# The last 256 rows' layernorm, issued between the older rows' down products

## The chip, the cores and the metric

The kernel runs on one core of one Trainium2 chip. The metric is the device time of a run in microseconds (us), given as a median over runs; less is better. The profile is one execution recorded by the hardware profiler. Its engines are called PE (TensorE matmul), PEld (TensorE weight load), DVE (VectorE), ACT (ScalarE), POOL (GpSimd) and SP (SyncE, which issues the DMAs of this kernel; SPq is its queue).

## The reference

One transformer block over 2048 rows of width 640, in bf16: a layernorm, attention with 32 heads of width 20, a residual, a second layernorm, a gated bilinear MLP of width 1728, and a second residual.

```python
def _layernorm(x, axis=-1, eps=1e-5):
    m = jnp.mean(x, axis=axis, keepdims=True)
    v = jnp.var(x, axis=axis, keepdims=True)
    return (x - m) / jnp.sqrt(v + eps)

h  = x + attention(_layernorm(x), A_wqkv, A_wo)   # 32 heads, softmax over 2048 keys
ln = _layernorm(h)
h2 = h + ((ln @ B_w_gate) * (ln @ B_w_up)) @ B_w_down
```

## The kernel before

**Tiling.** Rows go in blocks of 512 (four blocks, numbered 0 to 3), each of four tiles of 128 rows. Attention fills most of the span: score products on PE, exponentials on ACT (with a share of them done on DVE), value products on PE. A planner written in Python fills the gaps of that stream with jobs: projections, output products, and for the older rows the second layernorm and the MLP. It is a generator per job; a job yields between pieces of work, and the planner keeps clocks of its own to decide where a piece goes. The order is fixed when the program is built: each engine then runs its own list of instructions in that order.

**The end.** When the attention of block 3 is done, what is left cannot be spread over gaps any more. Its rows come in two halves: tiles 0 and 1 ("the older rows" here, 256 rows) are ahead, and tiles 2 and 3 (`LAST_T`, 256 rows) are last, since their attention ends last. The function `last_tail` (L1334) writes out the end by hand, after a pool `fin` of five PSUM buffers of one bank each (the tiles named `f`) has been opened. In the kernel before its steps are:

1. For each of the two last tiles, output products with the residual put in by an identity matmul (`out_most`, L1344 and L1346, `out_last`, L1350), into four `f` buffers. Between them the last head group is normalised (L793, L808, L1359).
2. For each of the two tiles, ACT copies the sums to SBUF (L1368), DVE takes mean and variance (`bn`, L219 and L220), and `rstd_act` (L921 to L934) makes the scale: small DVE instructions, a square root on ACT (L929), a reciprocal on DVE (L933).
3. `fill()` (L1383) runs what the planner has left. Here that is `job_y` of the older rows (L1272): four sets of 14 down products each (two row tiles by two halves of 320 columns; the matmuls are recorded at the helper `by_cols`, L286). Each set ends with one DVE addition to the residual (L1284), and after the second half of a tile a store of the tile goes out through SP's queue (L1291).
4. `ln_apply` (L243) on DVE subtracts the mean and scales, for both last tiles, giving the tiles `ln`.
5. `job_T` (L319) for both: five 128x128 transposes on PE (L323) into one `f` buffer, and one copy on ACT (L255) to `ln2T`.
6. Two weight tiles, `E`, are loaded through SP's queue (`w_tile`, L1187) for the MLP's third slice of columns; the other slices lie in SBUF or were asked for earlier.
7. `job_glu` (L1223) makes the MLP's up and gate products of the last rows (L1214, 140 matmuls, in slices 3, 4, 5, 6, 0, 1, 2); ACT copies up (L255), DVE multiplies it with gate (L1246, L1239) into `hh`. `flag` (L1388) checks the softmax sums.
8. `job_y` of the last rows: again four sets of 14 down products, four additions, and four stores of half a tile (L1289).

An `f` buffer is taken anew each time by `bank()` (L311), in turn; its taker waits until the reader of its last contents is done.

The helper that step 3 calls:

```python
    def fill():
        while peek() is not None:
            if cur["need"] != WAIT:
                run_slot()
```

`peek` (L509) tells whether a job is left, and `run_slot` (L537) runs one piece of it up to the point where its PSUM bank is closed, so that one call of `run_slot` is one set of 14 down products with its addition.

Of the kernel before, what the change touches and what calls it, by code (L numbers as in the profile page):

```python
# [87 lines left out]
def kernel(  # L88
# [91 lines left out]
    fill = []  # L180
# [61 lines left out]
    def ln_apply(dst, src, m32, r, k):  # L242
        nc.vector.tensor_scalar(dst, src, m32[:, k:k + 1], r[:, k:k + 1], ALU.subtract, ALU.mult)  # L243
# [9 lines left out]
    def evac(eng, dst, src):  # L253
        if eng == "act":
            nc.scalar.copy(dst, src)  # L255
        else:
            nc.vector.tensor_copy(dst, src)  # L257
# [19 lines left out]
    def mm(ns, kind="cols"):  # L277
        to(kind)
        clk["pe"] += ns
        clk["piece"] = ns  # L280
# [10 lines left out]
    def ev(n, slot=None):  # L291
        dve_op(n / 0.96 + 75, clk["pe"] + 150)
        slot = ring["cur"] if slot is None else slot
        ring["free"][slot] = clk["dve"] + WAKE
        if ring["busy"] == slot:
            ring["busy"] = None
# [7 lines left out]
    def ring_tile(dt=F32, w=BANK):  # L304
        k = ring["cur"] = next_slot()
        ring["order"].remove(k)
        ring["order"].append(k)
        clk["pe"] = max(clk["pe"], ring["free"][k])
        return mip.tile([P, w], dt, name="mi", tag=f"mi{k}")

    def bank(dt=F32, w=BANK):  # L311
        if end["pool"] is None:
            ps = ring_tile(dt, w)
            held["slot"] = ring["busy"] = ring["cur"]
            return ps
        ps = end["pool"].tile([P, BANK], F32, name="f", tag="f")
        return ps if dt == F32 else ps[:].bitcast(dt)[:, 0:w]

    def job_T(ln, dst, eng="dve", given=None, after=None):  # L319
        yield 60 * KT  # L320
        ps = bank(BF16, D) if given is None else given
        for c in range(KT):
            nc.tensor.transpose(ps[:, c * P:(c + 1) * P], ln[:, c * P:(c + 1) * P], ident[:])  # L323
        mm(60 * KT, "turn")
        if after:
            after()
        evac(eng, dst, ps[:].rearrange("p (c k) -> p c k", k=P))
        if given is None:
            ev(D // 2, held["slot"])
# [117 lines left out]
    for s, (p, g, lo, hi, _) in enumerate(segs):  # L447
        n = BANK // PASS[p][2]
# [50 lines left out]
    def advance():  # L499
        try:  # L500
            v = next(cur["gen"])
        except StopIteration:
            done.add(cur["key"])
            cur.update(key=None, gen=None, need=None, mid=False)
            return
        cur["mid"] = v is None
        cur["need"] = v

    def peek():  # L509
        if cur["mid"]:  # L510
            return 0
        if urgent and not (cur["key"] and cur["key"][0] == "nf"):
            if cur["gen"] is not None:
                jobs.appendleft((cur["key"], cur["gen"], cur["need"]))
            cur["key"], cur["gen"], cur["need"] = urgent.popleft()
        while cur["need"] is None or cur["need"] == WAIT:
            if cur["gen"] is None:
                if not jobs:
                    return None
                cur["key"], cur["gen"], cur["need"] = jobs.popleft()  # L520
                if cur["need"] not in (None, WAIT):
                    continue
            advance()
            if cur["need"] == WAIT:
                if cur["key"][0] == "nf" and jobs and not forced["on"]:
                    urgent.appendleft((cur["key"], cur["gen"], WAIT))
                    cur["key"], cur["gen"], cur["need"] = jobs.popleft()
                    continue
                other = None if forced["on"] else next((j for j in jobs if j[0] in needs and needs[j[0]] <= done), None)
                if other is None:  # L530
                    return WAIT
                jobs.remove(other)
                jobs.appendleft((cur["key"], cur["gen"], WAIT))
                cur["key"], cur["gen"], cur["need"] = other
        return cur["need"]

    def run_slot(limit=None):  # L537
        advance()
        while cur["mid"] and (limit is None or clk["pe"] <= limit):
            advance()  # L540
# [248 lines left out]
    def sums_to_rows(asb, w, ps=None):  # L789
        n = w // SLOT  # L790
        ps = bank() if ps is None else ps
        for t in range(w // P):
            nc.tensor.matmul(ps[:, HPG * t:HPG * (t + 1)], lhsT=asb[:, t * P:(t + 1) * P], rhs=late["if"][:, DH:P:SLOT], start=True, stop=True)  # L793
        mm(400, "turn")
        rr = nrm.tile([P, 2, NS], F32, name="rr", bufs=3)
        r16, ri = rr[:, 0, 0:n], rr[:, 1, 0:n]
        nc.vector.reciprocal(ri, ps[:, 0:n])
        bc = bc_tile(w)
        nc.vector.tensor_copy(bc[:, 0:w].rearrange("p (j e) -> p j e", e=SLOT), ri.rearrange("p (j e) -> p j e", e=1).to_broadcast([P, n, SLOT]))
        nc.vector.tensor_copy(r16, ps[:, 0:n])  # L800
        note_sums(rr, n)
        ev(w, held["slot"])
        return bc

    def rows_to_cols(bc, w, ps=None):
        ps = bank() if ps is None else ps
        for t in range(w // P):
            nc.tensor.matmul(ps[:, t * P:(t + 1) * P], lhsT=bc[:, t * P:(t + 1) * P], rhs=late["if"][:], start=True, stop=True)  # L808
        mm(800, "turn")
        return ps  # L810
# [373 lines left out]
    def w_tile(src, fp, wt):  # L1184
        w = min(FPW, FF - fp * FPW)
        view = wt[:, 0:KT * FPW].rearrange("p (c f) -> p c f", f=FPW)
        nc.sync.dma_start(view[:, :, 0:w], src[:, fp * FPW:fp * FPW + w].rearrange("(c p) f -> p c f", p=P))  # L1187
        return view
# [141 lines left out]
    def run(gen):  # L1330
        for _ in gen:
            pass

    def last_tail():  # L1334
        st = tail_st[LAST_B]
        on = On[LAST_B % 2]
        asb = final["asb"]
        c0 = LAST_T[0] * P
        ps_h = {}

        def out_most(t, hf):
            ps = ps_h[t, hf] = bank()
            cs = slice(hf * HALF, (hf + 1) * HALF)
            nc.tensor.matmul(ps[:, 0:HALF], lhsT=ident[:], rhs=st["xr"][t][:, cs], start=True, stop=False)  # L1344
            for g in range(NG - 1):
                nc.tensor.matmul(ps[:, 0:HALF], lhsT=on[g][:, t * P:(t + 1) * P], rhs=wo[g][:, cs], start=False, stop=False)  # L1346

        def out_last(t):
            for hf in range(2):
                nc.tensor.matmul(ps_h[t, hf][:, 0:HALF], lhsT=on[NG - 1][:, t * P:(t + 1) * P],  # L1350
                                 rhs=wo[NG - 1][:, hf * HALF:(hf + 1) * HALF], start=False, stop=True)
        ta, tb = LAST_T
        out_most(ta, 0)
        bc = sums_to_rows(asb, HW, ring_tile())
        out_most(ta, 1)
        ps = rows_to_cols(bc, HW, ring_tile())
        for k in range(2):
            cs = slice(k * P, (k + 1) * P)
            nc.vector.tensor_tensor(on[NG - 1][:, c0 + k * P:c0 + (k + 1) * P], asb[:, cs], ps[:, cs], ALU.mult)  # L1359
        out_most(tb, 0)  # L1360
        out_last(ta)
        out_most(tb, 1)
        out_last(tb)
        got = {}
        for t in LAST_T:
            mv = small.tile([P, 1, 2], F32, name="mv")
            for hf in range(2):
                nc.scalar.copy(st["xr"][t][:, hf * HALF:(hf + 1) * HALF], ps_h[t, hf][:, 0:HALF])  # L1368
            bn(mv, 0, None, [ps_h[t, hf][:, 0:HALF] for hf in range(2)])
            got[t] = rstd_act(mv, 1)  # L1370
        fill()
        ls = {}
        for t in LAST_T:
            ls[t] = late["s"].tile([P, D], BF16, name="ln2")
            ln_apply(ls[t][:], st["xr"][t][:], *got[t], 0)
        for t in LAST_T:
            run(job_T(ls[t], st["ln2T"][:, :, t * P:(t + 1) * P], "act"))
        st["w", 2] = [w_tile(src, 2, e_tile(0)) for src in (B_w_up, B_w_gate)]
        run(job_glu(st, LAST_T, tuple(range(RES0, FP)) + tuple(range(RES0))))
        flag()  # L1380
        run(job_y(st, LAST_T, True))

    def fill():  # L1383
        while peek() is not None:
            if cur["need"] != WAIT:
                run_slot()

    def flag():  # L1388
        le = dp.tile([P, DW], I16, name="dt", bufs=2)[:].bitcast(BF16)[:, 0:2 * NS]
# [171 lines left out]
```

## Time and profile before

| what | value |
|---|---|
| median of 3 runs | 879.17 us |
| lowest, highest run | 877.38 us, 884.9 us |
| span of the profiled execution (first to last instruction) | 875.8 us |
| PE, ACT, DVE busy over the span | 827.1, 799.6, 701.5 us |
| PE from 820 to 868 us, the end of the program | 44.17 of 48.00 us busy |

No time of its own is listed for the profiled execution beside its span; what lies around the span is in the runs' times and not in the profile. The median run stands 3.4 us above the span.

How to read it: the rows of the timeline give the start in us from the span's start, the length in us, the engine, the line, the operation with output and input, and the count of merged instructions; in square brackets stands how long the engine was idle before and which instruction ended that. The chain of work that ended last is followed back from the end: each row is a stretch in which that engine's work, or an "issue" gap, held the end. In a table by stretches, PEclk is the clock that was granted to TensorE as a share of full speed, and the DMA columns are the share of the 16 DMA engines and GB/s.

### The profile page before, as it was taken

The page shows a single profiled execution, that of the slowest core. Times are in us where ns is not written, and L with a number is a line of the kernel's source. Part 1 is how long each engine was busy: PE and PEld are TensorE (multiplying, and loading weights), DVE is VectorE, ACT ScalarE, POOL GpSimd, SP SyncE. Part 2 cuts the span into 40 slices and gives each one's busy share as a digit, 9 for nine tenths or more (in the row PEclk, how much of TensorE's full clock was granted, in tenths as well). Part 3 has the DMA queues.
Part 4 walks back from the last instruction along what each step waited for, and adds up shares of the span by engine and source line. Part 5 has one row for each costly group of instructions (what it writes and reads, how often), then busy time and mean ns, then how long its engine had stood idle before and what let it go on. Part 6 is the DMA issues. An engine that isn't in the chain of part 4 may idle for free.

```text
span 875.8 us, 34459 instructions
## 1 busy us (share of the span) xinstructions
PE 827.1 (94%) x15313; PEld 406.3 (46%) x15313; DVE 701.5 (80%) x1384; ACT 799.6 (91%) x711; POOL 191.0 (22%) x259
## 2 busy tenths in 40 slices
PE   8899999998999999999999999999999999999995
PEld 5334334332334334445444555655454556555774
DVE  6675778899778989888888888989988898788632
ACT  5899999999999999999999999999999999899530
POOL 2220001344413322212230223122310232014000
PEclk9999999999999999999999999999999999899998
DMA  6111230144222322101314031413510310031310
GB/s 183 35 59 52 68 98 3 44 120 114 53 67 53 115 74 76 39 9 39 98 40 128 24 98 45 117 31 97 127 34 23 99 48 15 17 93 48 82 46 18
DMA packets 93959, 57.62 MB, mean 66 GB/s; under 512 B 24236, under 2 KB 91692, under 8 KB 93804
## 3 DMA queue, kind: packets, MB, share of 16 engines
q1 hardware_dynamic: 93804, 55.36, 23.7%
q8 instruction: 121, 1.98, 0.9%
q14 instruction: 34, 0.28, 0.1%
HBM read 46.94 MB, written 8.16 MB: 63 GB/s over the span
## 4 chain that ended last, share of the span: by engine, by line
PE 46%; ACT 25%; DVE 19%; issue 5%; DMA 2%; SPq 1%; POOL 1%; ACTq 0%; DVEq 0%; POOLq 0%
ACT E L732 25%; PE sc L724 11%; PE acc L871 9%; PE mi L286 9%; PE mi L1214 8%; DVE di L744 5%; PE mi L360 3%; DVE di L632 2%; DVE dm L627 2%; DVE st L219 2%; PE f L286 2%; PE f L1214 2%; DVE dt L629 2%; PE mi L724 1%; PE acc L1421 1%
## 5 line engine op out<-in xcount | busy, mean ns | idle before, releaser
L732 ACT ACTIVATE E<-sc 128x1536 bf16<-128x1536 f32 (+1 forms) x679 | 782.5, 1271 | 23.6 <-PE sc L724 10.6
L744 DVE TENSOR_SCALAR di<-mi 128x512 int16<-128x512 f32 x350 | 238.1, 685 | 65.9 <-PE mi L724 61.8
L871 PE MATMUL acc<-E,vx 128*32 128x256 bf16 (+1 forms) x2532 | 221.4, 315 | 2.6 <-DVE vx L257 2.0
L724 PE MATMUL sc<-qa,kT 21*128 21x256 bf16 (+1 forms) x1800 | 205.2, 320 | 15.0 <-ACT E L732 10.1
L724 PEld LDWEIGHTS <-kT 21*128 21x128 bf16 x3072 | 85.6, 92 | 218.9 <-issue 208.7
L769 POOL TENSOR_TENSOR rr<-rr,powers 128x8 f32<-128x8 f32 (+1 forms) x44 | 95.9, 2180 | 407.0 <-DMA rr<-sums 406.9
L871 PEld LDWEIGHTS <-vx 128*32 128x32 bf16 x3612 | 81.5, 95 | 105.7 <-issue 95.0
L632 DVE TENSOR_TENSOR di<-di,dm 128x1024 bf16<-128x1024 bf16 x175 | 122.2, 698 | 4.6
L724 PE MATMUL mi<-qa,kT 21*128 21x256 bf16 (+1 forms) x376 | 98.0, 311 | 2.4 <-DVE di L744 1.3
L627 DVE TENSOR_SCALAR dm<-di 128x1024 int16<-128x1024 int16 x175 | 77.7, 444 | 3.7
L871 PE MATMUL acc<-dt,vx 128*32 128x256 bf16 (+1 forms) x540 | 78.1, 311 | 0.5 <-DVE dt L629 0.4
L871 PE MATMUL acc<-di,vx 128*32 128x256 bf16 (+1 forms) x540 | 77.8, 308 | 0.8 <-DVE di L632 0.6
L629 DVE TENSOR_SCALAR dt<-di 128x1024 int16<-128x1024 int16 x175 | 76.2, 436 | 0.0
L724 PE MATMUL sc<-qb,kT 21*128 21x256 bf16 (+1 forms) x732 | 67.1, 291 | 2.8 <-ACT E L732 2.4
L286 PE MATMUL mi<-wd,hh 128*32 128x320 bf16 x1344 | 63.5, 305 | 0.4 <-DVE hh L1239 0.2
L1214 PE MATMUL mi<-ln2T,wg 128*32 128x256 bf16 (+1 forms) x1170 | 55.6, 298 | 1.9 <-DVE di L744 1.0
L1214 PE MATMUL mi<-ln2T,wu 128*32 128x256 bf16 (+1 forms) x1170 | 54.6, 298 | 0.9 <-DVE di L744 0.5
L286 PEld LDWEIGHTS <-hh 128*32 128x32 bf16 (+1 forms) x1456 | 46.1, 98 | 18.0 <-issue 7.5
L1214 PEld LDWEIGHTS <-wg 128*32 128x32 bf16 (+1 forms) x1190 | 32.6, 96 | 13.7 <-issue 10.0
L286 PE MATMUL mi<-kT,ident 128*32 128x512 bf16 x528 | 37.0, 382 | 1.7 <-DVE di L744 1.6
L1214 PEld LDWEIGHTS <-wu 128*32 128x32 bf16 (+1 forms) x1190 | 32.4, 96 | 13.3 <-issue 9.3
L257 DVE CAST u<-mi 128x512 bf16<-128x512 f32 x49 | 33.5, 683 | 4.9 <-PE mi L1214 4.8
(134 smaller groups left out, 794.1 us busy)
## 6 DMA issues: line engine op xcount, KB each, us to landing
wu<-in_B_w_up_dram SPq DMA_DIRECT2D x29, 320.0 KB
wg<-in_B_w_gate_dram SPq DMA_DIRECT2D x29, 320.0 KB
dense<-dn SPq DMA_DIRECT2D x36, 128.0 KB
bc<-scr SPq DMA_DIRECT2D x64, 64.0 KB
bc<-scr SPq DMA_DIRECT2D x112, 32.0 KB
xr<-in_A_x_dram SPq DMA_DIRECT2D x16, 160.0 KB
out_dram<-xr SPq DMA_DIRECT2D x14, 160.0 KB
wd<-in_B_w_down_dram SPq DMA_DIRECT2D x13, 160.0 KB
```

What stands on the lines that cost most here:

```text
L257: nc.vector.tensor_copy(dst, src)
L286: nc.tensor.matmul(out[k:k + w, :], lhsT=lhsT[:, k:k + w], rhs=rhs, **flags)
L360: nc.tensor.matmul(ps[k:k + SLOT, :], lhsT=wqk_half(c, col // HALF)[:, m, col % HALF:col % HALF + SLOT], rhs=lnT[:, c, ch * QB:(ch + 1) * ...
L627: nc.vector.tensor_scalar(m16[:, 0:n], s16, M_MASK, M_BITS, ALU.bitwise_and, ALU.bitwise_or)
L629: nc.vector.tensor_scalar(t16[:, 0:n], s16, E_MASK, E_BITS, ALU.bitwise_and, ALU.bitwise_or)
L632: nc.vector.tensor_tensor(sb[:, 0:n], sb[:, 0:n], mb[:, 0:n], ALU.mult)
L724: nc.tensor.matmul(dst[:, h * w:(h + 1) * w], lhsT=kT[g][SLOT * j:SLOT * j + VS, (kt + h) * P:(kt + h + 1) * P], rhs=q_of(g, b, c0, w)[SLO ...
L732: nc.scalar.activation(e[:, 0:n], sc[:, 0:n], ACT.Exp, bias=EXP_BIAS, scale=SM_SCALE)
L744: nc.vector.tensor_scalar(t[:, k * BANK:(k + 1) * BANK], sd[:], EXP_A, 0.0, ALU.mult, ALU.max)
L769: nc.gpsimd.tensor_tensor(ri, r16, powers[:, 1:2].to_broadcast([P, n]), ALU.pow)
L871: nc.tensor.matmul(acc["t"][SLOT * j:SLOT * (j + 1), 0:w], lhsT=vx[kt][:, VS * h:VS * h + SLOT], rhs=e, start=(j not in acc["new"]), stop= ...
L1214: nc.tensor.matmul(ps[r0 + x:r0 + x + d, col:col + n], lhsT=wt[:, c, f0 + x:f0 + x + d], rhs=st["ln2T"][:, c, c0:c0 + n], start=(c == 0), ...
```

## The change

`fill` gets an optional count of pieces, and `last_tail` calls it three times: one set of the older rows' down products, then `ln_apply` for both last tiles, then two more sets, then the transposes of both last tiles with their ACT copies, then the rest, which is the fourth set. Nothing is computed otherwise, and no instruction is added or removed (DVE's list shows one row more only because four like rows in a row are split).

```diff
-        fill()
+        fill(1)
         ls = {}
         for t in LAST_T:
             ls[t] = late["s"].tile([P, D], BF16, name="ln2")
             ln_apply(ls[t][:], st["xr"][t][:], *got[t], 0)
+        fill(2)
         for t in LAST_T:
             run(job_T(ls[t], st["ln2T"][:, :, t * P:(t + 1) * P], "act"))
+        fill()
         st["w", 2] = [w_tile(src, 2, e_tile(0)) for src in (B_w_up, B_w_gate)]
...
-    def fill():
-        while peek() is not None:
+    def fill(n=None):
+        while n != 0 and peek() is not None:
             if cur["need"] != WAIT:
                 run_slot()
+                n = n and n - 1
```

On DVE, at the end of the two last tiles' statistics, with the old order marked - and the new one + (`xr` are the residual rows, `f` the PSUM buffers, `m` and `rstd` mean and scale, `hh` the MLP's product):

```order
 L927 TENSOR_SCALAR ve<-mvb 128x1
 L933 RECIPROCAL rstd<-den 128x1
-L1284 TENSOR_TENSOR xr<-f,xr 128x320 x4
-L243 TENSOR_SCALAR ln_21330<-xr,m_21239,rstd 128x640
-L243 TENSOR_SCALAR ln_21332<-xr,m_21256,rstd 128x640
+L1284 TENSOR_TENSOR xr<-f,xr 128x320
+L243 TENSOR_SCALAR ln_21280<-xr,m_21239,rstd 128x640
+L243 TENSOR_SCALAR ln_21282<-xr,m_21256,rstd 128x640
+L1284 TENSOR_TENSOR xr<-f,xr 128x320 x3
 L1246 TENSOR_TENSOR hh_19383<-f,u 128x2x256
```

The two `ln` instructions moved from behind the four additions to behind the first.

On PE, the kernel before, from the last product of the fourth set to the MLP's first product, each wait in brackets (`wd` is the down weight, `wres` an up or gate weight that lies in SBUF):

```order
L286 MATMUL f<-wd_5233,hh_19386 128x320
L323 LDWEIGHTS ln_21330 [waits DVE_49]
L323 MATMUL f<-ident,ln_21330 128x128
...
L323 MATMUL f<-ident,ln_21332 128x128
L1214 LDWEIGHTS wres
L1214 MATMUL f<-ln2T,wres 128x256 [waits Activation_49]
```

The transposes stand between the fourth set and the MLP, with a wait for DVE ahead of them and one for ACT behind them.

On PE, the changed kernel, from the last product of the third set to the MLP's first product:

```order
L286 MATMUL f<-wd_5233,hh_19386 128x320
L323 LDWEIGHTS ln_21280 [waits DVE_49]
L323 MATMUL f<-ident,ln_21280 128x128
...
L323 MATMUL f<-ident,ln_21282 128x128
L286 LDWEIGHTS hh_19380
L286 MATMUL f<-wd_5220,hh_19380 128x320
...
L286 MATMUL f<-wd_5233,hh_19386 128x320
L1214 LDWEIGHTS wres [waits DVE_49]
L1214 MATMUL f<-ln2T,wres 128x256 [waits Activation_49]
```

The same two waits are there, and the fourth set's 14 products now stand between the transposes and the wait for ACT. The first weight load of the MLP has gained a wait for DVE. Its `f` buffer is in both kernels the one that the second set filled; before, the wait for `ln` was behind the second set's addition on DVE and so covered it, and now that addition comes after `ln`. The fourth set takes the buffer of the first set. The lists of ACT, POOL and SP are the same before and after; on SP's, the older rows' two stores stand ahead of the two loads of `E` as they did.

## The prediction

> **What bounds the kernel now.** I read the page's busy times first, then the chain of work that ended last for the end of the program, then the timeline there, and then tables by stretches for the granted clock and the DMA. The page begins with the span and PE's share:
>
> ```profile
> span 875.8 us, 34459 instructions
> PE 827.1 (94%) x15313; PEld 406.3 (46%) x15313; DVE 701.5 (80%) x1384; ACT 799.6 (91%) x711; POOL 191.0 (22%) x259
> ```
>
> These shares are means over all stages, and the change touches only the end, so the end has to be read by itself. The chain in order of time (start, length, what held the end):
>
> ```profile
> 832.75 7.62 PE f L286 x56
> ...
> 840.40 0.04 DVE xr L1284
> 840.44 0.37 issue
> 840.80 0.45 DVE ln L243
> ...
> 841.30 0.47 PE f L323 x5
> ...
> 841.79 1.29 ACT ln2T L255 x2
> 843.09 0.04 issue
> 843.13 15.14 PE f L1214 x140
> ...
> 858.36 0.69 DVE hh L1246
> ...
> 859.58 7.73 PE f L286 x56
> ```
>
> The reader is to see that PE holds the end before 840.37 (832.75 + 7.62) and from 843.13 on, and that for the 2.76 us between (843.13 - 840.37) the work goes from PE to DVE, back to PE, to ACT and back to PE. In the timeline the same place shows what each engine did:
>
> ```profile
> 832.32 0.43 PE L1350 MATMUL f<-wo,part 128*128 128x320 bf16 x2
> 832.59 7.77 PE L286 MATMUL f<-wd,hh 128*128 128x320 bf16 x56
> 835.84 0.16 DVE L933 RECIPROCAL rstd<-den 128x1 f32<-128x1 bf16 x1 [0.27 <-ACT den L929]
> 835.92 0.47 DVE L1284 TENSOR_TENSOR xr<-f,xr 128x320 bf16<-128x320 f32 x1
> 836.60 0.49 DVE L1284 TENSOR_TENSOR xr<-f,xr 128x320 bf16<-128x320 f32 x1 [0.20 <-PE f L286]
> 838.50 0.49 DVE L1284 TENSOR_TENSOR xr<-f,xr 128x320 bf16<-128x320 f32 x1 [1.41 <-PE f L286]
> 840.40 0.49 DVE L1284 TENSOR_TENSOR xr<-f,xr 128x320 bf16<-128x320 f32 x1 [1.41 <-PE f L286]
> 840.80 0.80 DVE L243 TENSOR_SCALAR ln<-xr,m,rstd 128x640 bf16<-128x640 bf16 x2
> 841.30 0.81 PE L323 MATMUL f<-ident,ln 128*128 128x128 bf16 x10 [0.94 <-DVE ln L243]
> 843.13 8.58 PE L1214 MATMUL f<-ln2T,wres 128*128 128x256 bf16 x80 [1.02 <-ACT ln2T L255]
> ```
>
> The second scale was ready at 836.00 (835.84 + 0.16), yet `ln` began at 840.80. It stood in DVE's list behind four additions, the last of which waited for the fourth set of down products. So PE stood idle twice, 0.94 us ahead of the transposes and 1.02 us behind them, with no other work written between.
>
> **The change, part by part.** No instruction is added or taken away; three things move. The sum is made against the profiled execution.
>
> *The two `ln` go up on DVE.* They now follow the first addition, which ends at 836.39 (835.92 + 0.47). A pair takes 0.80 by its row, and the one seen began 0.09 before the end of the addition ahead of it (840.80 against 840.40 + 0.49), so both are done by about 837.2. Queued behind them on DVE is the second addition: it started at 836.60 and will start at 837.2, 0.6 late. The third is free to wait for PE as before. The buffer that the second addition frees is next used by the first up product after 840, three us later, so the lateness costs nothing there; without that cover it would cost 0.6.
>
> *The transposes go ahead of the fourth set.* The sets are 1.90 apart (838.50 and 840.40), so the third is done at 838.47 (840.37 - 1.90). `ln` is ready 1.3 us before that, so the first idle gap, 0.94, goes away. What ten transposes cost between matmuls is not shown here, where both sides were idle; it is shown elsewhere in the stream, as the time from their start to the start of the next matmul:
>
> ```profile
> 449.93 0.73 PE L323 MATMUL mi<-ident,ln 128*128 128x128 bf16 x10
> 450.60 0.39 PE L724 MATMUL sc<-qa,kT 21*128 21x512 bf16 x2
> ...
> 795.07 0.95 PE L323 MATMUL mi<-ident,ln 128*128 128x128 bf16 x10
> 795.95 0.28 PE L871 MATMUL acc<-E,vx 128*32 128x256 bf16 x1
> L323 PE MATMUL f<-ident,ln x10: 219/219/230, 841.3 to 841.9; 128*128 128x128 bf16 x10
> ```
>
> That is 0.67 at 449.93 and 0.88 at 795.07, with 0.81 for the ten at 841.30 between them.
>
> *The fourth set becomes the cover for ACT's copies.* The copies began 0.49 after the transposes began (841.30 to 841.79) and ended 1.78 after (843.08). With transposes from 838.47 on they end at 840.25. The fourth set is done at 840.37 plus the price of the transposes, 841.04 to 841.25. So the copies are hidden with 0.8 us to spare, and the second gap, 1.02, goes too. What is late next is the fourth set itself, that is PE. Its buffer was freed by the first addition, at 836.4, so it waits for nothing.
>
> *The sum.* The MLP's first product started at 843.13. At the dear end it starts at 841.25 (840.37 + 0.88), which gains 1.88. At the cheap end, matmuls follow each other before the modelled end of the one ahead: the down products began at 832.59, while the products before them end at 832.75 in the record (832.32 + 0.43), 0.16 later. Then it starts at 840.88 (840.37 - 0.16 + 0.67), which gains 2.25. I take 0.67 without the overlap, the row in which the ten ran in one row with matmuls on both sides: 841.04, a gain of 2.09. Nothing can gain more than the whole 2.76.
>
> *What follows the MLP's start.* The gain lasts to the end only if the following stretch is paced by PE. The stretches (PE, PEld, DVE, ACT, POOL busy, granted clock, DMA):
>
> ```profile
> 843.10:859.40 16.30, 15.13 (x140) 13.02 (x139) 5.28 (x10) 4.09 (x7) 0.00 (x0) 1.00 0.13 36
> 843.00:844.00 1.00, 0.87 (x9) 0.78 (x8) 0.00 (x0) 0.08 (x1) 0.00 (x0) 1.00 1.04 289
> 845.00:846.00 1.00, 1.00 (x12) 0.90 (x10) 0.42 (x1) 0.00 (x1) 0.00 (x0) 1.00 0.06 14
> ```
>
> PE works 15.13 of 16.30 us there, DVE 5.28 and ACT 4.09; the rest of PE's time is the wait for the last `hh` and the check of the sums, which comes with it. So everything from there on moves up together, the stores included.
>
> *SP's queue.* The older rows' second store waits for the fourth addition, which is late by the transposes' 0.67, and the two loads of `E` stand behind that store:
>
> ```profile
> 841.38 0.39 SPq L1187 DMA_DIRECT2D E<-in_B_w_up_dram  x1
> 841.87 0.54 SPq L1187 DMA_DIRECT2D E<-in_B_w_gate_dram  x1
> 855.91 2.35 PE L1214 MATMUL f<-ln2T,E 128*128 128x256 bf16 x20
> ```
>
> The DMA engines are full in the us after 843 and busy for 0.06 of the us after 845, so both tiles had landed by about 845.5. They land 0.7 later, at 846.2, and are first needed at 853.8 (855.91 - 2.09): 7.6 us of cover, so I cost this at nothing. The first store, 0.6 late, has nothing behind it until the second.
>
> **The rivals.** *The lead is given back.* PE could reach the end of the MLP 2 us sooner and then wait for something that was late anyway; the time would be 879.2. For it: the check of the sums stands behind the last `hh` on DVE. Against it: that DVE work is itself released by PE, and POOL, which feeds the check, shows 0.00 busy in that stretch.
>
> *Transposes cost their own length.* Each is recorded with 0.219 us. If ten in a busy stream cost 2.19 instead of 0.67, the fourth set ends at 842.56, the gain is 0.57 and the time 878.6. Against it stand the two rows in the stream. The Trainium skill, page "TensorE: Matmul & The Clock Gate", section "Part 4: PE-mode transpose", gives about 275 ns for a transpose of this size in a kernel; by that figure ten would take an estimated 2.75 us, the gain would be 0.01 and the time 879.2. The trace does not agree: 0.81 for ten at 841.30 is 81 ns each.
>
> *The clock falls in the end.* This one ends on the other side. The trace has one such fall, in full work:
>
> ```profile
> 748.00:751.00 3.00, 2.61 (x60) 1.30 (x54) 2.63 (x6) 2.80 (x4) 0.00 (x0) 1.00 0.00 0
> 751.00:754.00 3.00, 3.00 (x64) 1.66 (x58) 2.16 (x7) 3.00 (x4) 0.63 (x2) 0.93 0.02 5
> 754.00:757.00 3.00, 3.00 (x38) 1.90 (x36) 2.59 (x5) 2.21 (x3) 0.64 (x2) 0.50 0.01 3
> 757.00:760.00 3.00, 3.00 (x50) 1.45 (x46) 1.81 (x5) 1.70 (x3) 0.00 (x0) 0.50 0.00 0
> 760.00:765.00 5.00, 5.00 (x124) 2.63 (x116) 3.83 (x9) 4.70 (x5) 0.00 (x0) 0.96 0.12 39
> 840.40:843.10 2.70, 0.81 (x10) 0.62 (x11) 1.20 (x3) 1.29 (x2) 0.00 (x0) 1.00 0.37 92
> ```
>
> Half clock for about 6.8 us (0.4 + 3 + 3 + 0.4) costs 3.4 us where PE sets the pace. One such fall after 838 would give 880.5 (877.1 + 3.4); it decides the sign once it lasts over 4.2 us. For it: the fall came with PE busy, so busy work does not shield from it. Against it: the change takes idle time out of PE, and the end ran at 1.00 even across its two gaps. The same page, section "Part 1: The HAM clock gate", lets the clock halve after an idle window of about 3.4 us. By that rule no fall is due here, before or after, and the time stays 877.1. The trace bears it out for the gaps at 840, but the fall at 754 came after no more than 0.39 us of idle in three.
>
> **How the numbers follow.** The median run less the gain is 879.17 - 2.09 = 877.1; for the profiled execution the span should go from 875.8 to 873.7. The chances: the forecast 0.83, the lead given back 0.05, dear transposes 0.04, a fall of the clock 0.06, and 0.02 for what I don't see. The low end is the lowest run less the whole gap, 877.38 - 2.76 = 874.6. The high end is dear transposes with one fall more in the run, 878.6 + 3.4 = 882.0; this also takes in the scatter of the three runs, which is larger than the gain. Some 0.15 lies outside, most of it scatter. A measurement of this kernel can tell about 1% from no change, which is 8.8 us, and no case gains a third of that: faster 0.02. Slower by over 1% takes three falls at once or something unseen: 0.03. Within 1%: 0.95.
>
> **What would show it.** In the changed kernel's timeline the transposes should start at about 838.4 with no idle ahead of them, the fourth set should follow them at once, ACT's copies should end at about 840.2, and the MLP should start near 841.0 with no idle put down to ACT. The second addition should start at about 837.2, the loads of `E` at about 842. The forecast is wrong if PE shows a wait ahead of L323 or L1214 of over 0.3 us, if the step from the transposes to the fourth set is over 1 us, or if PE's idle time in the MLP's stretch, 1.17 us here (16.30 - 15.13), has grown by the time that was gained.

## The result

The changed kernel takes 876.27 us (median of 22 runs, 871.93 to 878.61), the one before 878.55 us (median of 22 runs, 874.37 to 884.9). The ratio is 0.9962 with a 95% interval of 0.9948 to 0.9976, so about 3.3 us less, between 2.1 and 4.6. It is not the quotient of the two medians, which lie 2.28 us apart (0.9974). The profiled execution spans 873.3 us where the one before spanned 875.8.

The chain of work that ended last, in the end of the changed kernel:

```profile
832.86 5.71 PE f L286 x42
838.56 0.56 PE f L323 x10
839.12 1.90 PE f L286 x14
841.02 14.98 PE f L1214 x140
...
856.09 0.69 DVE hh L1246
...
857.31 7.73 PE f L286 x56
```

From 832.86 to 856.00 (841.02 + 14.98) there is only PE. The rows of DVE `ln` and of ACT `ln2T`, with the gaps beside them, have left the chain. The timeline of the same place:

```profile
832.69 5.87 PE L286 MATMUL f<-wd,hh 128*128 128x320 bf16 x42
836.02 0.47 DVE L1284 TENSOR_TENSOR xr<-f,xr 128x320 bf16<-128x320 f32 x1
836.41 0.80 DVE L243 TENSOR_SCALAR ln<-xr,m,rstd 128x640 bf16<-128x640 bf16 x2
837.12 0.48 DVE L1284 TENSOR_TENSOR xr<-f,xr 128x320 bf16<-128x320 f32 x1
838.40 0.72 PE L323 MATMUL f<-ident,ln 128*128 128x128 bf16 x10
838.60 0.49 DVE L1284 TENSOR_TENSOR xr<-f,xr 128x320 bf16<-128x320 f32 x1 [0.99 <-PE f L286]
838.88 1.29 ACT L255 COPY ln2T<-f 128x640 bf16<-128x640 bf16 x2 [2.96 <-PE f L323]
838.96 2.06 PE L286 MATMUL f<-wd,hh 128*128 128x320 bf16 x14
840.86 8.58 PE L1214 MATMUL f<-ln2T,wres 128*128 128x256 bf16 x80
842.03 0.39 SPq L1187 DMA_DIRECT2D E<-in_B_w_up_dram  x1
865.06 0.49 DVE L1284 TENSOR_TENSOR xr<-f,xr 128x320 bf16<-128x320 f32 x1 [1.41 <-PE f L286]
```

No PE row carries an idle time in brackets up to the MLP. To compare executions whose earlier parts differ by a few us, I measure from the start of the older rows' down products. The MLP's first product came 10.54 us after it before (843.13 - 832.59) and comes 8.17 us after it now (840.86 - 832.69), which is 2.37 us less. From there to the last addition it is 24.20 us in both (867.33 - 843.13 and 865.06 - 840.86). The ratio would have it some 1 us more, the medians not; 2.37 us lies within the interval of the ratio, and the last experiment but one comes back to it.

### The profile page after: what moved, and what is told of

Same layout as the page of the kernel before. It is cut to its first block, busy times and chain, and to the rows that moved or that the text cites. A ratio compares the mean times of both kernels' runs of the same rounds, so it can differ in the third digit from the quotient of the medians.

```text
span 873.3 us, 34459 instructions
## 1 busy us (share of the span) xinstructions
PE 827.1 (95%) x15313; PEld 405.4 (46%) x15313; DVE 701.2 (80%) x1384; ACT 800.0 (92%) x711; POOL 192.4 (22%) x259
## 3 DMA queue, kind: packets, MB, share of 16 engines
HBM read 46.94 MB, written 8.16 MB: 63 GB/s over the span
## 4 chain that ended last, share of the span: by engine, by line
PE 44%; ACT 27%; DVE 18%; issue 5%; DMA 2%; SPq 1%; POOL 1%; DVEq 0%; ACTq 0%; POOLq 0%
ACT E L732 27%; PE sc L724 11%; PE acc L871 9%; PE mi L1214 8%; PE mi L286 7%; DVE di L744 5%; PE mi L360 3%; DVE di L632 2%; PE f L286 2%; DVE st L219 2%; DVE dm L627 2%; PE f L1214 2%; DVE dt L629 1%; PE mi L724 1%; DMA rr<-sums 1%
## 5 line engine op out<-in xcount | busy, mean ns | idle before, releaser
L724 PE MATMUL mi<-qb,kT 21*128 21x256 bf16 (+1 forms) x164 | 36.5, 290 | 1.1 <-DVE di L744 0.9
```

The lines of the kernel that those rows point to most:

```text
L724: nc.tensor.matmul(dst[:, h * w:(h + 1) * w], lhsT=kT[g][SLOT * j:SLOT * j + VS, (kt + h) * P:(kt + h + 1) * P], rhs=q_of(g, b, c0, w)[SLO ...
```

## The experiments

The theory is that the end of the program held two hand-offs in which PE had nothing to do, one for `ln` on DVE and one for the copies on ACT, that each part of the change removes one of them, and that the time so gained reaches the end since PE paces all that follows. The rivals are that one part alone brings it, that the lead is given back, and that transposes between matmuls cost their own recorded length.

**Only `ln` moved up.** The transposes stay behind the fourth set.

```diff
         fill(1)
...
             ln_apply(ls[t][:], st["xr"][t][:], *got[t], 0)
-        fill(2)
+        fill()
         for t in LAST_T:
             run(job_T(ls[t], st["ln2T"][:, :, t * P:(t + 1) * P], "act"))
-        fill()
```

> One part of the change alone: the two ln go ahead of the second addition on DVE, the transposes stay behind the fourth set. Measured from the start of the older rows' first down product to the start of the MLP's first product, which took 10.54 us before (832.59 to 843.13) and 8.17 in the changed kernel (832.69 to 840.86). My theory (two hand-offs, each worth its own idle time): the wait for ln goes, the wait for ACT's copies stays at about 1.0 us; transposes start 7.6 after the start of the sets, and the MLP 1.83 after them (as 841.30 to 843.13): 9.4 us, a gain of 1.1 on before. Rival A (only the cover for ACT's copies matters, DVE's order does not): 10.5 us, no gain. Rival B (the gain came from the order on DVE alone): 8.2 us. In the time: 0.1% less than before by my theory, which is at the edge of what five rounds tell.

The rows of PE and ACT in its timeline:

```profile
834.15 7.77 PE L286 MATMUL f<-wd,hh 128*128 128x320 bf16 x56
841.76 0.72 PE L323 MATMUL f<-ident,ln 128*128 128x128 bf16 x10
842.24 1.29 ACT L255 COPY ln2T<-f 128x640 bf16<-128x640 bf16 x2 [4.86 <-PE f L323]
843.58 8.58 PE L1214 MATMUL f<-ln2T,wres 128*128 128x256 bf16 x80 [1.10 <-ACT ln2T L255]
```

The transposes follow the sets without a wait, and the wait for ACT stands at 1.10 us. From the sets to the MLP it is 9.43 us (843.58 - 834.15), a gain of 1.11 on before where 1.1 was expected. Both rivals fall. The time's ratio, 0.9991 (0.9964 to 1.0018), can't tell 1.1 us from nothing; the rows can.

**Only the transposes moved up.** The `ln` stay behind the third addition.

```diff
-        fill(1)
+        fill(3)
         ls = {}
...
             ln_apply(ls[t][:], st["xr"][t][:], *got[t], 0)
-        fill(2)
         for t in LAST_T:
             run(job_T(ls[t], st["ln2T"][:, :, t * P:(t + 1) * P], "act"))
         fill()
```

> The other part alone: the transposes stand ahead of the fourth set, but the two ln stay behind the third addition on DVE. My theory: the third addition starts 5.9 us after the start of the sets (838.60 against 832.69), ln follows it, so PE waits about 1 us for ln ahead of the transposes, and then the fourth set covers ACT's copies: transposes at 6.8, the MLP at 6.8 + 0.56 + 1.90 = 9.3 us, a gain of 1.2 on before. The gains of the two parts add up to that of the whole, 2.4. Rival B (the order on DVE alone gives the gain): 10.5 us, no gain. Rival A (only the cover matters): 8.2 us, with no wait ahead of the transposes.

Its timeline, PE and the DVE rows ahead of the transposes:

```profile
837.68 5.87 PE L286 MATMUL f<-wd,hh 128*128 128x320 bf16 x42
843.59 0.49 DVE L1284 TENSOR_TENSOR xr<-f,xr 128x320 bf16<-128x320 f32 x1 [1.41 <-PE f L286]
844.00 0.79 DVE L243 TENSOR_SCALAR ln<-xr,m,rstd 128x640 bf16<-128x640 bf16 x2
844.49 0.81 PE L323 MATMUL f<-ident,ln 128*128 128x128 bf16 x10 [0.94 <-DVE ln L243]
845.14 2.06 PE L286 MATMUL f<-wd,hh 128*128 128x320 bf16 x14
847.04 8.58 PE L1214 MATMUL f<-ln2T,wres 128*128 128x256 bf16 x80
```

The other wait is back, 0.94 us for `ln`, and the one for ACT is gone. From the sets to the MLP it is 9.36 us, a gain of 1.18. The two parts together make 2.29 (1.11 + 1.18), the whole 2.37: they add up to within 0.1 us. Neither rival's figure, 8.2 or 10.5 us, came. The time's ratio, 0.9986 (0.9958 to 1.0014), again can't tell the gain from nothing.

**The transposes twice.** The changed kernel, with each of the end's transposes issued twice into the same place.

```diff
-        for c in range(KT):
+        for c in list(range(KT)) * (1 if end["pool"] is None else 2):
             nc.tensor.transpose(ps[:, c * P:(c + 1) * P], ln[:, c * P:(c + 1) * P], ident[:])
```

> The changed kernel with each of the ten transposes of the end issued twice into the same buffer, which costs their price in the stream once more. My theory: ten cost 0.56 to 0.67 us among other matmuls, so the MLP starts 8.17 + 0.6 = 8.8 us after the start of the sets, with ACT's copies still hidden. Rival (transposes cost their own recorded length of 0.219 us): 8.17 + 2.2 = 10.4 us. The Trainium skill, page TensorE: Matmul & The Clock Gate, section Part 4: PE-mode transpose, by its 275 ns would give an estimated 10.9 us.

Two rows of its chain, and the MLP's start with that of the sets in its timeline:

```profile
842.92 1.12 PE f L323 x20
844.03 1.90 PE f L286 x14
```

```profile
837.05 5.87 PE L286 MATMUL f<-wd,hh 128*128 128x320 bf16 x42
...
845.77 8.58 PE L1214 MATMUL f<-ln2T,wres 128*128 128x256 bf16 x80
```

Twenty take 1.12 us, so ten take 0.56 again, 56 ns each, though each is recorded with 219 ns. The MLP starts 8.72 us after the sets where 8.8 was expected. The price by the length of a row falls, and so, for this stream, does the 275 ns of the Trainium skill (page "TensorE: Matmul & The Clock Gate", section "Part 4: PE-mode transpose"). That section gives its figure for one transpose in the context of another kernel; what counts here is from start to start. This kernel was run once, at 879.77 us, and the experiment rests on its rows alone.

**The cover of the loads taken away.** The changed kernel, with the slice in `E` first in the MLP instead of last.

```diff
-        run(job_glu(st, LAST_T, tuple(range(RES0, FP)) + tuple(range(RES0))))
+        run(job_glu(st, LAST_T, (2,) + tuple(range(RES0, FP)) + tuple(range(2))))
```

> The changed kernel with the cover of the two loads of E taken away: the MLP takes the slice whose weights are in E first instead of last. The loads are issued 842.03 and 842.53 in the changed kernel, 1.2 us after the MLP's first product. My theory (the loads take about 4 us from the first issue until both have landed, and had 7 to 8 us of cover): PE stands idle for 4 to 5 us ahead of the MLP, and the first product comes about 12.5 us after the start of the sets instead of 8.17. Two theories on the clock after that idle time. One, from the Trainium skill, page TensorE: Matmul & The Clock Gate, section Part 1: an idle window of about 3.4 us lets the granted clock fall to half, so the MLP's first 3 to 7 us run at 0.5 and the MLP takes about 2 to 3 us longer than 15.1. The other, that falls in this kernel come without regard to idle time, as at 754 in the profile before: the clock stays at 1.00 and the MLP takes 15.1.

Its timeline, and then the stretches ahead of the MLP and in it (the granted clock is the third figure from the end of a row):

```profile
831.28 5.87 PE L286 MATMUL f<-wd,hh 128*128 128x320 bf16 x42
840.62 0.39 SPq L1187 DMA_DIRECT2D E<-in_B_w_up_dram  x1
844.08 3.71 PE L1214 MATMUL f<-ln2T,E 128*128 128x256 bf16 x20 [4.47 <-DMA E<-in_B_w_up_dram]
```

```profile
839.60:844.08 4.48, 0.01 (x1) 0.00 (x1) 0.49 (x1) 0.00 (x0) 0.00 (x0) 0.93 0.64 174
844.08:846.00 1.92, 1.92 (x10) 1.36 (x11) 0.00 (x0) 0.00 (x0) 0.00 (x0) 0.50 0.08 20
846.00:848.00 2.00, 2.00 (x16) 1.64 (x15) 0.10 (x1) 0.58 (x1) 0.00 (x0) 0.78 0.00 0
848.00:850.00 2.00, 2.00 (x21) 1.80 (x19) 0.59 (x1) 0.58 (x1) 0.00 (x0) 1.00 0.00 0
```

PE stands idle for 4.47 us, and the MLP starts 12.80 us after the sets (12.5 expected). The first load takes 3.46 us from issue to use (844.08 - 840.62). In the changed kernel it is issued at 842.03 and the slice is used from 853.6 on, so the cover there is some 8 us, where the prediction had 7.6. The two theories on the clock part here: it fell to half near the end of the idle time, for about 3.4 us in all (0.07/0.5 of 4.48, then 1.92, then 0.22/0.5 of 2.00), and the MLP's 140 products took 16.50 us in the chain instead of 14.98; that is 1.5 more and not the 2 to 3 expected, as 0.6 us of the fall lay in the idle time. The fall is what the Trainium skill (page "TensorE: Matmul & The Clock Gate", section "Part 1: The HAM clock gate") says of an idle window of about 3.4 us. It was seen in one run (879.52 us); that it fell there by chance is unlikely, since no other profile has a fall in this stretch, but is not excluded.

**The changed kernel again.** It differs in nothing from the changed kernel.

> The changed kernel once more, beside before on one chip, since its ratio so far (0.9962, or 3.3 us) is larger than the 2.4 us that its profile shows in the end of the program. My theory (the rest is scatter from falls of the clock further up): 0.9973, or 2.4 us, within the interval, and the profile again shows 8.17 us from the start of the sets to the MLP. Rival (the change brings something outside the end as well): 0.9962 or less again.

The ratio is 0.9968 (0.9940 to 0.9996), 876.28 us against 878.08. Its profile has the sets at 831.92 and the MLP at 840.08:

```profile
831.92 5.87 PE L286 MATMUL f<-wd,hh 128*128 128x320 bf16 x42
...
840.08 8.58 PE L1214 MATMUL f<-ln2T,wres 128*128 128x256 bf16 x80
...
864.29 0.49 DVE L1284 TENSOR_TENSOR xr<-f,xr 128x320 bf16<-128x320 f32 x1 [1.41 <-PE f L286]
```

That is 8.16 us, within 0.01 us of the first profile, and the last addition again comes 32.37 us after the start of the sets (864.29 - 831.92). The ratio lies between the 0.9973 and the 0.9962 that the two theories gave and its interval holds both, so the ratio doesn't tell them apart; the medians lie 1.80 us apart.

What does tell more is the mean granted clock, which is on record for each run of this comparison. Most of the scatter goes with it: a straight line through the times of this chip's 47 runs of three kernels (before, the changed kernel and the last one below), with one offset for each kernel, drops 0.67 us for each 0.001 of the clock. By this estimate the changed kernel, at an equal clock, is 2.3 us under before (1.7 to 3.0), which agrees with the 2.37 us of the rows and speaks against the rival. Whether the change alters the falls of the clock themselves is not shown.

**The next hand-off.** In the changed kernel PE still waits 1.16 us for the check of the sums ahead of the last down products. Here the check goes on DVE behind `ln` and on PE ahead of the transposes, and the last down products take the slices in the order in which the MLP makes them.

```diff
+        ok = flag_sums()
         fill(2)
+        flag(ok)
...
-        flag()
-        run(job_y(st, LAST_T, True))
+        run(job_y(st, LAST_T, True, tuple(range(2 * RES0, 2 * FP)) + tuple(range(2 * RES0))))
...
-                for f in range(2 * FP):
+                for f in fs:
```

> The changed kernel with the next hand-off of the same kind taken away: the check of the softmax sums is made on DVE behind ln and on PE ahead of the transposes, and the last rows' down products take the MLP's slices in the order in which they were made, so that the slice made last is used last. In the changed kernel PE stands idle 1.16 us ahead of the check's product at 857.15, and that product and its step to the next cost 0.1. My theory (a wait of PE in the end is worth its own length): the down products follow the MLP without a gap, and the last addition comes 1.2 to 1.5 us sooner after the start of the MLP's first product: 22.8 us instead of 24.20 (840.86 to 865.06), a span of about 872 us. Rival (the lead is given back, since the end waits for something that is not on PE): the span stays at 873.3. In the time: 0.4% less than before.

> The kernel of e5_flag_early once more on the same chip as e6_after_again, to compare the two directly. My theory: 1.2 us (0.14%) under e6_after_again, 0.9959 of before, and 31.1 us from the start of the sets to the last addition, where e6_after_again has 32.4. Rival (the lead is given back after the end of the program's work): the same time as e6_after_again.

The end of the chain in the second of these runs, and then the start of its sets and its last addition in the timeline:

```profile
843.87 0.09 PE f L1401
843.96 0.67 PE f L323 x10
844.63 1.90 PE f L286 x14
846.53 14.96 PE f L1214 x140
861.49 7.62 PE f L286 x56
869.12 0.02 issue
869.14 0.49 DVE xr L1284
```

```profile
838.00 5.87 PE L286 MATMUL f<-wd,hh 128*128 128x320 bf16 x42
...
846.37 8.58 PE L1214 MATMUL f<-ln2T,wres 128*128 128x256 bf16 x80
...
869.14 0.49 DVE L1284 TENSOR_TENSOR xr<-f,xr 128x320 bf16<-128x320 f32 x1 [1.41 <-PE f L286]
```

PE is the chain from the first set to the last product, with no gap at all. In both profiles it is 31.14 us from the start of the sets to the last addition (867.45 - 836.31 and 869.14 - 838.00), against 32.37 in both of the changed kernel, so 1.23 us less, as expected. From the MLP's start it is 22.77 us (869.14 - 846.37) where 22.8 was expected. The span of about 872 us did not come: the two profiles span 876.0 and 877.4 us, as their sets begin 3.6 and 5.3 us later than in the changed kernel, so the spans by themselves tell nothing of the end. In the time: 876.64 us and a ratio of 0.9957 (0.9930 to 0.9985) in the first run; in the second 875.25 us and 0.9951 (0.9925 to 0.9978), on the same chip as the repeated changed kernel's 876.28. The intervals overlap with those of the changed kernel, so the ratios can't tell the two versions apart; on the one chip that ran both, the medians lie 1.03 us apart. At an equal clock, by the estimate above, this version is 1.2 us under the changed kernel (0.5 to 1.9), so the lead was not given back. This version beats both kernels in its rows, and the kernel before by its intervals as well.

## Why the prediction was right

**What bounds the end.** PE with two holes: right. Both holes are gone from the chain, and each comes back when its part of the change is undone.

**The `ln` on DVE.** Forecast done at about 837.2 and the second addition at 837.2; the rows have 837.21 (836.41 + 0.80) and 837.12. The late second addition held up nobody.

**ACT's copies under the fourth set.** Forecast over by 840.25, with 0.8 us to spare; they ended at 840.17 (838.88 + 1.29), 0.7 before the MLP.

**The size.** Forecast 2.09 us in the end of the program, measured 2.37, which is more than even the cheap end of the sum, 2.25. The term that was off is the price of the ten transposes: I took 0.67 from the row at 449.93 and left out the 0.16 by which matmuls overlap the modelled end of those before. Measured, the ten cost 0.56 from start to start (838.40 to 838.96), and the overlap is there (the fourth set's record ends at 841.02, the MLP starts at 840.86). That makes 0.11 and 0.16, so 0.27 of the 0.28 that were missing. Why the row at 449.93 has 0.67 is open.

**The time.** 877.1 was forecast and 876.27 measured, so 0.8 us too much. Most of it is the base: the forecast took off from a median of 3 runs, 879.17, and the median of 22 is 878.55. That the absolute time came so close has some luck in it, as single runs of the changed kernel lie up to 6.7 us apart; what bears the theory out are the rows. The span of the profiled execution was forecast at 873.7 and came out at 873.3. The 3.4 us between the span and the median of before were of two kinds: in a run of the changed kernel the time of 875.08 us stands 1.8 us over its span of 873.3, and with the same 1.8 the profiled execution of before took an estimated 877.6, which is 1.6 under the median of three.

**The rivals.** The lead was not given back: 24.20 us from the MLP's start to the last addition in both. Transposes at their own length fell by the doubling. A fall of the clock in the end came in one of the nine profiles, that in which PE was made to wait for the loads; the stretch from 830 to 864 us shows 1.00 in the other eight. The argument that I put beside that rival was half wrong: I held the fall at 754 against the rule on idle windows, but with an idle time of 4.47 us the fall came as the rule says, in the one run that has such a gap in the end. Why the clock fell at 754 with PE's rows nearly full is open.

## What to carry to other kernels

Look in the chain for the places where work changes engine several times in a few us with no other work of the waiting engine written between; independent work that is already in the list can be split so that part of it stands behind each hand-off, and the gain is the sum of the holes that it fills, as long as the same engine paces what follows. Price a short matmul in a stream from its start to the start of the next, not from its own length. A change worth 0.1 to 0.3% is told by the rows of the stage it touches long before the medians of the times tell it.

## What was not expected of the hardware

The scatter of the runs goes with the granted clock. Runs of the changed kernel with a mean clock of 0.998 and 0.986 took 871.93 and 877.56 us, a difference of more than twice the 2.37 us of the rows. In the profiles these are falls to half clock of several us in the middle of the program, at places that come again: near 215 us and near 630 us in five each of the nine profiles told here, and near 475, 665 and 755 us in two or three each; six have one near 15 to 25 us too. The second run of the last experiment has one near 215 and one near 475, each behind a stretch in which PE was idle for more than 1 us of 5:

```profile
210.00:215.00 5.00, 2.99 (x40) 0.91 (x37) 4.96 (x7) 3.73 (x4) 4.23 (x6) 0.97 0.59 145
215.00:220.00 5.00, 5.00 (x42) 1.07 (x38) 4.28 (x8) 2.72 (x3) 0.00 (x0) 0.50 0.62 135
...
470.00:475.00 5.00, 3.83 (x70) 1.45 (x64) 4.93 (x10) 4.25 (x4) 1.32 (x2) 0.92 0.59 155
475.00:480.00 5.00, 5.00 (x100) 2.43 (x94) 2.28 (x4) 3.21 (x4) 0.00 (x0) 0.74 0.17 45
```

Its profiled run took 879.27 us, 4 us above the median of that kernel's runs, with the shortest end of all. PE has no gap left in that end up to its last product, so the falls further up are the next place to look; what starts them was not tried.
